# Heads in groups of four, bands of a sub-block in one operation, and softmax pieces between the blocks

## The chip, the cores and the metric

One core of a Trainium2 chip. The time is the device time of one execution in microseconds (us). Runs of the kernel before lie between 759.1 and 761.6 us. Engines are called as in the profile: PE is TensorE with PEld its weight loads, DVE is VectorE, ACT is ScalarE, POOL is GpSimd, SP is SyncE, which here only starts transfers.

## The reference

A causal convolution of seven taps whose weights are made per token and head by a softmax, then a feed-forward layer with a squared ReLU:

```python
# x (8, 4096, 192), weight_gen (8, 4096, 8 heads, 7 taps)
w = softmax(weight_gen, axis=-1)
out = np.einsum('bshk,bskhg->bshg', w, x_unf)      # x_unf: x at t-6 .. t, 24 channels a head
h = np.maximum(out.reshape(32768, 192) @ w_in, 0)  # w_in  (192, 2048)
return h * h @ w_out                               # w_out (2048, 192)
```

## The kernel before

The 32768 tokens are 64 sub-blocks of 512. From the second block on, a block is two sub-blocks. TensorE alternates between 16 units of the first product ("u"), the sums of the second product for the block before ("M") and one convolution ("C") for the block after:

```python
steady = "MuMuuu" * 3 + "MuuuMCu"
```

The convolution is done as a matrix product with banded matrices. DVE builds the bands of a sub-block from the softmax rows `wr` and a mask; they stand in `bd` by pairs of heads, so that the two heads of a pair alternate:

```python
def st_band(j, tiles):                       # tiles of 104 columns; called with (0,1), (2,3), (4,)
    shape = (P, HP * len(tiles), n // SL, 2 * SL)          # HP = H // 2
    nc.vector.tensor_tensor(out=bd_t[j][...], in0=wr_t[j][...].broadcast_to(shape),
                            in1=mask[...].broadcast_to(shape), op=AluOp.mult)

# st_conv: 120 matmuls a block, four side by side on different columns of the array
bd = bd_t[s][:, H * lo : H * hi].rearrange("p (g c e) -> p g e c", g=HP, e=2)
nc.tensor.matmul(out=yps[k // per][p0 : p0 + m, col + a : col + b],
                 lhsT=x_t[s][:, i, 32 * q : 32 * q + m],
                 rhs=bd[:, h // 2, h % 2, a - lo : b - lo],    # every second element: step two
                 start=True, stop=True, tile_position=(0, p0))
```

The softmax is made in pieces of eight rows (`exp` on ACT; `total`, `recip` and `scale` on DVE), placed at certain units of certain blocks. `exp` writes the heads of a group next to each other, `total` therefore reads the taps of one head at the step of the group, and `scale` needs one operation a group. The second product ends in `o_sum`, a copy on ACT and an add on DVE; there is one pair of PSUM buffers for it.

The softmax here doesn't subtract the row's maximum and nothing guards it: scores larger than these inputs give would overflow.

Of the kernel before, what the change touches and what calls it, by code (L numbers as in the profile page):

```python
# [9 lines left out]
def kernel(  # L10
# [25 lines left out]
    nc = tc.nc  # L36
# [5 lines left out]
    Dff = moe_w_in.shape[1]  # L42
    Dm = moe_w_out.shape[1]
    HK = H * KK
    HP = H // 2

    P = 128
    TB = 512
# [39 lines left out]
    NQ = Dff // WQ  # L88
    w_i = const.tile([P, WQ, 2, NQ + NQ // 2], f16, name="w_i")
    w_o = const.tile([P, NF, Dm], f16, name="w_o")  # L90
    mask = const.tile([P, P, 2], f16, name="mask")
    FIRST = 8
    PARTS = {0: (8, 8, 8, 8), 1: (8, 8, 16), 2: (16, 16)}
    v_big = const.tile([P, R + 2 * HALO, HP, SL, 2], f16, name="v_big")
    v_first = [
        const.tile([P, FIRST + 2 * HALO, HP, SL, 2], f16, name=f"v_first{i}") for i in (0, 1)
    ]

    def band_mask():

        nc.gpsimd.memset(mask, 1.0)
        for sign, base in ((1, 0), (-1, KK - 1)):
            nc.gpsimd.affine_select(
                out=mask, in_=mask, pattern=[[sign, P], [0, 2]], compare_op=AluOp.is_ge,
                fill=0.0, base=base, channel_multiplier=-sign,
            )

# [38 lines left out]
    class Softmax:  # L146
# [35 lines left out]
        def exp(self, lo, hi):  # L182

            if lo == 0:
                self.ex = self.tile(p_one, p_one, "ex", HK, "ex8").rearrange(
                    "p (r g k e) -> p r g k e", g=HP, k=KK, e=2
                )
                self.ssum, self.rcp = (
                    self.tile(p_sm, p_sm, n, H, n + "8").rearrange(
                        "p (r g e) -> p r g e", g=HP, e=2  # L190
                    )
                    for n in ("ssum", "rcp")
                )
            nc.scalar.activation(  # L194
                out=self.ex[:, lo:hi].rearrange("p r g k e -> p (r g) k e"),
                in_=self.wg[:, lo:hi].rearrange("p r (g e) k -> p (r g) k e", e=2),
                func=ActF.Exp,
            )

# [10 lines left out]
        def scale(self, lo, hi, eng):  # L210

            v = self.v
            while lo < hi:
                n = min(SL - lo % SL, hi - lo)
                for g in range(HP):
                    eng.tensor_tensor(  # L216
                        out=bass.AP(
                            tensor=v.tensor,
                            offset=v.offset + lo * H * SL + lo % SL * 2 + g * SL * 2,
                            ap=[list(v.ap[0]), [H * SL + 2, n], [H * SL, KK], [1, 2]],  # L220
                        ),
                        in0=self.ex[:, lo : lo + n, g],
                        in1=self.rcp[:, lo : lo + n, g].unsqueeze(2).broadcast_to((P, n, KK, 2)),
                        op=AluOp.mult,
                    )
                lo += n
# [64 lines left out]
        copy(out=x_t[j].rearrange("p t d -> p (t d)"), in_=x_st[j][:, 0 : NT * D])  # L291

    def wr_load(j):
        wr_t[j] = p_wr.tile([P, NT, HP, SL * 2], f16, name="wr")
        wr = wr_t[j].rearrange("p t g c -> p t (g c)")
        block_load(j, wr, vd_t[j // NBB], H * SL, nc.sync)

    def wr_load_sbuf(j, parts, order, engines):

        wr_t[j] = p_wr.tile([P, NT, HP, SL * 2], f16, name="wr")  # L300
        n = 0
        for i in order:
            t0 = max(j % NBB * TB + tile_start(j, i), 0)
            for s in parts:
                a, b = max(t0, s.t0), min(t0 + P, s.t0 + P * s.r)
                if a < b:
                    engines[n % len(engines)].dma_start(  # L307
                        out=wr_t[j][a - t0 : b - t0, i].rearrange("p g c -> p (g c)"),
                        in_=s.v[
                            (a - s.t0) // s.r : (b - s.t0) // s.r, HALO : HALO + s.r  # L310
                        ].rearrange("p r g c e -> p r (g c e)"),
                    )
                    n += 1

    def st_band(j, tiles):

        if j not in bd_t:
            bd_t[j] = p_bd.tile([P, H * TB], f16, name="bd")
        i = tiles[0]
        lo, hi, n = bounds[i], bounds[tiles[-1] + 1], bounds[i + 1] - bounds[i]  # L320
        shift = 0 if i == 0 and j % NBB == 0 else lo - tile_start(j, i)
        shape = (P, HP * len(tiles), n // SL, 2 * SL)
        nc.vector.tensor_tensor(  # L323
            out=bd_t[j][:, H * lo : H * hi].rearrange(
                "p (g m c) -> p g m c", g=shape[1], c=2 * SL
            ),
            in0=wr_t[j][:, i : tiles[-1] + 1]
            .rearrange("p t g c -> p (t g) c")
            .unsqueeze(2)
            .broadcast_to(shape),  # L330
            in1=mask[:, shift : shift + n]
            .rearrange("p (m c) e -> p m (c e)", c=SL)
            .unsqueeze(1)
            .broadcast_to(shape),
            op=AluOp.mult,
        )
# [35 lines left out]
    def st_conv(j):  # L372
# [7 lines left out]
            ps_h.tile([P, 2 * TB], f32, name="yp", tag="h") for _ in range(-(-NK // per))  # L380
        ]
        for later, s, i, q, half, a, b, base in conv_pieces(j):
            lo, hi = bounds[i], bounds[i + 1]
            _, ha, hb, pre = quads[q]
            m, h = (32, hb) if later else (pre, ha)
            bd = bd_t[s][:, H * lo : H * hi].rearrange("p (g c e) -> p g e c", g=HP, e=2)
            p0 = RT * half + 32 * (q % 2)
            k = q // 2
            col = th * (k % per) - base
            nc.tensor.matmul(  # L390
                out=yps[k // per][p0 : p0 + m, col + a : col + b],
                lhsT=x_t[s][:, i, 32 * q : 32 * q + m],
                rhs=bd[:, h // 2, h % 2, a - lo : b - lo],
                start=True,
                stop=True,
                skip_group_check=True,
                tile_position=(0, p0),
            )
# [72 lines left out]
            ],  # L471
        )

    def st_bands(j, part):

        groups = ((0,), (1,), (2, 3)) if j % NBB == 0 else ((0, 1), (2, 3))
        for tiles in (groups, ((NT - 1,),))[part]:
            st_band(j, tiles)

    with nc.allow_low_precision("fp16 matmul pipeline"), tc.manual_schedule():  # L480

# [54 lines left out]
        for i in (0, 2, 1, 3, 4):  # L536
            st_band(0, (i,))
        st_conv(0)
        s1.exp(0, s1.rh)
        st_bands(1, 0)  # L540
        st_bands(1, 1)
        x_cast(1, nc.vector.tensor_copy)
        s1.total(0, s1.rh)
        s1.recip(0, s1.rh)
        s1.scale(0, s1.rh, nc.vector)

        nc.gpsimd.memset(x_st[1][:, 0:1], 0.0)
        for q in range(4):
            load_w_out(q, 4)
        move_rows(s1)  # L550
        s2.load(nc.sync)
        nc.gpsimd.memset(v_big, 0.0)
        x_load(2)
        x_load(3)



# [7 lines left out]
        def at(j, u, kind, *args):  # L565
# [2 lines left out]
        PIECE = 8  # L568

        TIMES = {  # L570
            (0, 2): ((1, 7), (2, 1)),
            (0, 3): ((2, 15), (3, 1)),
            (1, 0): ((3, 15), (4, 1)),
            (1, 1): ((4, 15), (5, 1)),
            (1, 2): ((5, 9), (5, 15), (6, 1)),
            (2, 0): ((6, 15), (7, 1), (7, 9)),
            (2, 1): ((8, 1), (8, 15), (9, 1)),
            (3, 0): ((9, 9), (9, 15), (10, 9), (10, 15), (11, 1)),
        }

        EXP_AT = {1: 0, 7: 4, 9: 4, 15: 8}
        loads = {}
        for n, s in enumerate(parts[2:], 2):
            b, f = s.b, s.fb
            k = n - min(m for m, p in enumerate(parts) if p.b == b)
# [2 lines left out]
            )  # L588
            pieces = [(lo, min(lo + PIECE, s.rh)) for lo in range(0, s.rh, PIECE)]
            for (j, u), (lo, hi) in zip(times, pieces, strict=True):  # L590
                at(j, EXP_AT[u], "exp", s, lo, hi)
                at(j, u, "soft", s, lo, hi)
            if n > 2:
                loads.setdefault(times[0][0] - 1, []).append(s)
        for j in range(1, NBLK - 1):
            a = BLOCKS[j + 1][0]
            when = (1, 9, 5, 9)
            if j == 1:
                when = (1, 1, 3, 3)
            elif j == 2:  # L600
                when = (5, 6, 8, 9)
            elif j in (3, 4, 5):
                when = (5, 7, 9, 11)
            elif j == 6:
                when = (9, 9, 11, 11)
            for u, args in zip(when, ((a, 0), (a, 1), (a + 1, 0), (a + 1, 1))):
                at(j, u, "band", *args)

        stored, waiting = set(), []

# [11 lines left out]
        def run_fill(j, u):  # L622
            for kind, *args in fill.get((j, u), ()):
                if kind == "band":
                    st_bands(*args)
                    continue
                s, lo, hi = args
                if kind == "exp":
# [18 lines left out]

        FCS = (range(NF // 2), range(NF // 2, NF))
        for j, (sub, n) in enumerate(BLOCKS):
            for s in loads.get(j, ()):  # L650
                s.load(nc.sync)
            if j + 2 < NBLK:
                load_rows(j + 2)
            u = m = 0
            for step in orders.get(j, steady):
# [13 lines left out]
                    u += 1  # L669
                elif j + 1 < NBLK:  # L670
                    st_conv(j + 1)
            if 0 < j < NBLK - 2:
                for k in range(BLOCKS[j + 2][0], sum(BLOCKS[j + 2])):
                    x_load(k)

# [46 lines left out]
```

## Time and profile before

| | |
|---|---|
| time, median | 760.98 us |
| span of the profiled run | 759.8 us |
| packed block (convolution to convolution) | 22.55 us |
| convolution, 120 matmuls | 1.59 us |
| DVE busy | 631.2 us |

The instruction groups of the kernel before that the change touches (line, engine, operation, out<-in, shapes, count, then busy time and mean ns of one, then idle time before):

```profile
L323 DVE TENSOR_TENSOR bd<-wr,mask 128x1664 f16<-128x1664 f16 x119 | 116.5, 1018 | 2.2 <-DMA wr<-v_first 2.2
...
L390 PE MATMUL yp<-bd,xt 128*32 128x104 f16 x1524 | 36.2, 210 | 0.0
...
L216 DVE TENSOR_TENSOR v_big<-ex,rcp 128x112 f16<-128x112 f32 x104 | 21.7, 272 | 1.0
...
L194 ACT ACTIVATE ex<-wg 128x448 f32<-128x448 f32 x30 | 19.0, 633 | 0.0
...
L201 DVE TENSOR_REDUCE ssum<-ex 128x64 f32<-128x448 f32 x30 | 18.3, 610 | 0.0
```

The bands, the scale and the sum are on DVE (116.5, 21.7 and 18.3 us in these shapes, beside 337 us of squares), the exponential on ACT. The second line is on TensorE, which sets the time; its mean of 210 ns is one matmul from its start to its end, while the matmuls of a convolution follow each other every 11.6 ns, (1.59 - 0.21) us / 119. What a matmul costs is this distance to the next, which has to be read from the timeline: a row of n matmuls there contains n - 1 distances and one last matmul.

### The profile page before, as it was taken

The numbers are of one execution on the slowest core, as the hardware profiler recorded it, in microseconds if no ns is written. First come the engines' busy times: TensorE is split into PE (matmuls) and PEld (weight loads), VectorE is DVE, ScalarE is ACT, GpSimd is POOL, SyncE is SP. The second block draws the span as 40 slices with busy tenths as digits, with TensorE's granted clock in tenths as the row PEclk, the third lists the DMA queues.
The fourth block names the chain that finished last, engine by engine and source line by source line (L and its number), as shares of the span: only waits on it lengthen the run. The fifth ranks groups of instructions, "written<-read, shape, count | busy, mean of one in ns | idle before, by whom it ended". The sixth has DMA issues, their size and how long they took to land.

```text
span 759.8 us, 33723 instructions
## 1 busy us (share of the span) xinstructions
PE 741.8 (98%) x15266; PEld 561.0 (74%) x15266; DVE 631.2 (83%) x1119; ACT 623.8 (82%) x753; POOL 87.3 (11%) x126
## 2 busy tenths in 40 slices
PE   7899999999999999999999999999999999999998
PEld 3767777877877777777777777777777777777777
DVE  5888999898899988898888888888888887777853
ACT  3887888878888888888888888888888888888873
POOL 3522212011100110010100110001100011000000
PEclk9999999999999999999999999999999999999999
DMA  7844432546325544344445423454432454432311
GB/s 228 121 79 97 91 96 51 100 104 138 70 68 114 107 79 59 107 76 82 79 79 116 96 60 52 79 136 98 68 63 41 76 107 79 58 68 52 52 44 65
DMA packets 122395, 65.23 MB, mean 86 GB/s; under 512 B 83881, under 2 KB 118668, under 8 KB 121740
## 3 DMA queue, kind: packets, MB, share of 16 engines
q1 hardware_dynamic: 78012, 46.46, 21.4%
q0 software_dynamic: 44096, 16.53, 20.1%
q8 instruction: 119, 1.95, 1.1%
q14 instruction: 24, 0.20, 0.1%
q10 hardware_dynamic: 144, 0.10, 0.0%
HBM read 48.61 MB, written 28.70 MB: 102 GB/s over the span
## 4 chain that ended last, share of the span: by engine, by line
PE 87%; DVE 5%; issue 2%; DMA 1%; ACT 1%; POOL 0%; SPq 0%; POOLq 0%; DVEq 0%
PE o L447 42%; PE h L415 39%; PE yp L390 5%; DVE g L427 2%; DVE bd L323 1%; DMA xt<-in_x_dram 1%; DVE o_sb L462 1%; DMA wr<-v_first 0%; ACT o_sb L461 0%; ACT t L424 0%; DVE v_big L216 0%; DVE rcp L208 0%; DVE ssum L201 0%; POOL xt L277 0%; POOL xt L271 0%
## 5 line engine op out<-in xcount | busy, mean ns | idle before, releaser
L424 ACT ACTIVATE t<-h 128x1024 f16<-128x1024 f32 x512 | 497.1, 1026 | 72.7 <-PE h L415 71.0
L427 DVE TENSOR_TENSOR g<-t 128x1024 f16<-128x1024 f16 x512 | 336.7, 688 | 97.9 <-ACT t L424 96.0
L447 PEld LDWEIGHTS <-g 64*128 64x128 f16 x8192 | 351.5, 94 | 61.4 <-issue 9.7
L447 PE MATMUL o<-w_o,g 64*128 64x192 f16 x8192 | 384.9, 243 | 5.9 <-DVE o_sb L462 5.3
L415 PE MATMUL h<-y,w_i 64*128 64x512 f16 (+1 forms) x3168 | 378.8, 371 | 6.9 <-ACT t L424 5.1
L415 PEld LDWEIGHTS <-w_i 64*128 64x128 f16 x3168 | 164.5, 94 | 118.8 <-issue 9.4
L323 DVE TENSOR_TENSOR bd<-wr,mask 128x1664 f16<-128x1664 f16 (+2 forms) x201 | 158.2, 830 | 4.7 <-DMA wr<-v_first 4.7
L277 POOL DMA_DIRECT2D xt<-in_x_dram x62 | 51.3, 830 | 442.4 <-PE yp L390 419.5
L461 ACT COPY o_sb<-o 128x384 f32<-128x384 f32 x129 | 62.2, 482 | 33.0 <-PE o L447 33.0
L462 DVE TENSOR_TENSOR o_sb<-o,o_sb 128x384 f32<-128x384 f32 x129 | 71.3, 553 | 12.5 <-ACT o_sb L461 7.1
L401 ACT CAST y<-yp 128x1024 f16<-128x1024 f32 (+1 forms) x64 | 48.1, 802 | 15.3 <-PE yp L390 15.3
L390 PE MATMUL yp<-bd,xt 128*32 128x104 f16 (+8 forms) x3864 | 51.9, 208 | 0.2
L390 PEld LDWEIGHTS <-xt 128*32 128x32 f16 (+3 forms) x3864 | 46.1, 92 | 6.5 <-issue 5.4
L194 ACT ACTIVATE ex<-wg 128x448 f32<-128x448 f32 (+2 forms) x44 | 27.2, 618 | 6.6 <-DMA wg<-in_weight_gen_dram 6.6
L201 DVE TENSOR_REDUCE ssum<-ex 128x64 f32<-128x448 f32 (+2 forms) x44 | 26.2, 595 | 3.9 <-ACT ex L194 3.9
L216 DVE TENSOR_TENSOR v_big<-ex,rcp 128x112 f16<-128x112 f32 (+1 forms) x136 | 27.4, 265 | 1.2
L208 DVE RECIPROCAL rcp<-ssum 128x64 f32<-128x64 f32 (+2 forms) x44 | 23.7, 539 | 1.5
L307 POOL DMA_DIRECT2D wr<-v_first x31 | 16.9, 563 | 28.2 <-DVE v_first L216 28.2
L267 POOL DMA_DIRECT2D xt<-in_x_dram x7 | 3.8, 546 | 137.6 <-PE yp L390 137.6
L508 PE MATMUL wp<-warm 128*128 128x512 f16 x42 | 12.1, 459 | 1.3 <-DVE warm L500 1.3
L508 PEld LDWEIGHTS <-warm 128*128 128x128 f16 x42 | 4.7, 114 | 8.1 <-issue 3.8
L216 DVE TENSOR_TENSOR v_first<-ex,rcp 128x112 f16<-128x112 f32 (+1 forms) x48 | 9.1, 256 | 0.3
(17 smaller groups left out, 23.9 us busy)
## 6 DMA issues: line engine op xcount, KB each, us to landing
out_dram<-o_sb SPq DMA_DIRECT2D x63, 384.0 KB, 2.7
xt<-in_x_dram POOLq DMA_DIRECT2D x42, 240.0 KB, 6.0
wg<-in_weight_gen_dram SPq DMA_DIRECT2D x4, 1064.0 KB, 8.0
xt<-in_x_dram POOLq DMA_DIRECT2D x20, 192.0 KB, 6.4
wr<-vd SPq DMA_DIRECT2D x38, 80.0 KB, 5.3
vd<-v_big SPq DMA_DIRECT2D x5, 512.0 KB, 5.7
wg<-in_weight_gen_dram SPq DMA_DIRECT2D x6, 392.0 KB, 4.3
wg<-in_weight_gen_dram SPq DMA_DIRECT2D x3, 616.0 KB, 6.1
```

The lines of the kernel that those rows point to most:

```text
L194: nc.scalar.activation(out=self.ex[:, lo:hi].rearrange("p r g k e -> p (r g) k e"), in_=self.wg[:, lo:hi].rearrange("p r (g e) k -> p (r g ...
L216: eng.tensor_tensor(out=bass.AP(tensor=v.tensor, offset=v.offset + lo * H * SL + lo % SL * 2 + g * SL * 2, ap=[list(v.ap[0]), [H * SL + 2, ...
L277: eng.dma_start(out=dst[:, first:last], in_=ap)
L323: nc.vector.tensor_tensor(out=bd_t[j][:, H * lo : H * hi].rearrange("p (g m c) -> p g m c", g=shape[1], c=2 * SL), in0=wr_t[j][:, i : tile ...
L390: nc.tensor.matmul(out=yps[k // per][p0 : p0 + m, col + a : col + b], lhsT=x_t[s][:, i, 32 * q : 32 * q + m], rhs=bd[:, h // 2, h % 2, a - ...
L401: nc.scalar.copy(out=y[:, k0:k1, 0:th], in_=yp[:, 0 : (k1 - k0) * th].rearrange("p (k c) -> p k c", c=th),)
L415: nc.tensor.matmul(out=h[:, half, jj * th : (jj + 1) * th], lhsT=w_in_chunk(u * per + jj, slot, half), rhs=y_t[j][r0 : r0 + RT, k, 0:th], ...
L424: nc.scalar.activation(out=t1, in_=h, func=ActF.Relu)
L427: nc.vector.tensor_tensor(out=g, in0=t1, in1=t1, op=AluOp.mult)
L447: nc.tensor.matmul(out=oo[:, cc * Dm : (cc + 1) * Dm], lhsT=g[r0 : r0 + RT, cc * P : (cc + 1) * P], rhs=w_o[r0 : r0 + RT, fc, :], start=(f ...
L461: nc.scalar.copy(out=o_sb, in_=o[0][:, c])
L462: nc.vector.tensor_tensor(out=o_sb, in0=o[1][:, c], in1=o_sb, op=AluOp.add)
```

## The change

The intent: fewer and longer operations on DVE (one band operation for a sub-block instead of three, two scale operations a piece instead of four), softmax pieces away from the places where the add of the second product has to wait for them, and a start in which ACT is not held up by the second softmax part. The groups of four are what halves the number of scale operations. Cut to the core:

```diff
-    HP = H // 2
+    HE = 4
+    HG = H // HE
 ...                                    # 2 -> HE and HP -> HG in mask, v_big, wr, exp, total, scale
-            bd_t[j] = p_bd.tile([P, H * TB], f16, name="bd")
+            bd_t[j] = p_bd.tile([P, H * NT * STEP], f16, name="bd")
 ...
-            bd = bd_t[s][:, H * lo : H * hi].rearrange("p (g c e) -> p g e c", g=HP, e=2)
+            bd = bd_t[s][:, H * lo : H * hi].rearrange("p (g c e) -> p g e c", g=HG, e=HE)
-                rhs=bd[:, h // 2, h % 2, a - lo : b - lo],
+                rhs=bd[:, h // HE, h % HE, a - lo : b - lo],
 ...
-        groups = ((0,), (1,), (2, 3)) if j % NBB == 0 else ((0, 1), (2, 3))
-        for tiles in (groups, ((NT - 1,),))[part]:
-            st_band(j, tiles)
+        for tiles in (range(first), range(first, last), range(last, NT)):
+            if tiles:
+                st_band(j, tiles)
 ...                                    # the start
-        s1.exp(0, s1.rh)               # now before unit 4 of block 0
-        s1.total(0, s1.rh); s1.recip(0, s1.rh); s1.scale(0, s1.rh, nc.vector)   # now before unit 5
-        nc.gpsimd.memset(x_st[1][:, 0:1], 0.0)
         for q in range(4):
             load_w_out(q, 4)           # now earlier on its queue
-        move_rows(s1)
-        s2.load(nc.sync)               # now at unit 6 of block 0
-        x_load(2); x_load(3)           # now after block 0
 ...                                    # softmax pieces: unit 1 -> unit 0 in most places, others moved;
                                        # bands at units 1 and 5 (5 and 9 early on) instead of 1, 5, 9, 9
```

## The prediction

Numbers from the traces: 11.6 ns from matmul to matmul in the convolution; a clock of 0.83 in the window from 20 to 30 us, which holds the stop of 4.17 us, and 0.63 after the one of 1.48; and 0.52 ns for an element of the bands. The sum: 1 (start) + 1 (block 2 to 3) + 4 (blocks 5 to 10) = 6 us off 760.6, so 754.6, stated as 754, with the convolution at 0.

Three of its figures, with what the traces show beside them. The 42.7 ns of rival A are the 102.4 columns of a mean matmul: a matmul of 512 columns takes 377 ns and one of 192 columns 243, so (377 - 243)/320 = 0.42 ns a column and 42.9 ns. The 0.117 us under *Scale* are 112 elements: the operation takes 272 ns for 112 and, in the changed kernel, 388 for 224, so 0.116 us. The 1.7 us of lost clock are an estimate from the 0.63: after that stop 31 matmuls of the second product took 2.53 us and six of the first 1.58, elsewhere 1.48 (for 31 or 32) and 0.82.

> **What bounds the kernel now.** I read the page first, then the timeline of TensorE, then the waits and the timelines of VectorE (DVE) and ScalarE (ACT) where TensorE stood still, and last a table of windows for its clock. From the page:
>
> ```profile
> span 759.8 us, 33723 instructions
> PE 741.8 (98%) x15266; PEld 561.0 (74%) x15266; DVE 631.2 (83%) x1119; ACT 623.8 (82%) x753; POOL 87.3 (11%) x126
> ...
> PE 87%; DVE 5%; issue 2%; DMA 1%; ACT 1%; POOL 0%; SPq 0%; POOLq 0%; DVEq 0%
> ```
>
> TensorE is busy 98% of the span and carries 87% of the chain that ended last; DVE, which nearly all of the change is about, carries 5%. So a DVE instruction saved is worth only what TensorE waits for DVE. A busy PE need not be a dense one, so the timeline of TensorE decides (start, duration, engine, line, shape, count, idle before):
>
> ```profile
> 405.25 1.59 PE L390 MATMUL yp<-bd,xt 128*32 128x104 f16 x120
> 406.78 0.82 PE L415 MATMUL h<-y,w_i 64*128 64x512 f16 x6
> 407.43 1.48 PE L447 MATMUL o<-w_o,g 64*128 64x192 f16 x32
> ...
> 427.80 1.59 PE L390 MATMUL yp<-bd,xt 128*32 128x104 f16 x120
> ```
>
> From one convolution to the next is 22.55 us. A block holds 16 units of the first product at 0.647 us (1.94 us for three), 8 half sums of the second at 1.32 and one convolution of about 1.6: 10.35 + 10.56 + 1.6 = 22.5. An ordinary block is packed, and no saving on DVE can shorten it. What can be won is in blocks that take longer. I subtracted 22.55 from the distance between successive convolutions: the block from 56.98 us has 3.96 too much, those from 128.60, 152.13, 176.69, 200.18 and 245.78 have 0.98, 2.01, 0.94, 0.52 and 0.55 (5.0 together), the remaining ones 0.0 to 0.6. Most of the latter (2.0 us in all) show "issue" before a matmul and no other engine, about every 90 us, so I leave them as they are. The stops, with what ended them:
>
> ```profile
> 21.45 2.74 PE L415 MATMUL h<-y,w_i 64*128 64x256 f16 x24 [4.17 <-ACT t L424]
> ...
> 61.42 2.53 PE L447 MATMUL o<-w_o,g 64*128 64x192 f16 x31 [1.48 <-DVE o_sb L462]
> ...
> 131.77 1.48 PE L447 MATMUL o<-w_o,g 64*128 64x192 f16 x31 [0.65 <-DVE o_sb L462]
> ...
> 155.53 1.48 PE L447 MATMUL o<-w_o,g 64*128 64x192 f16 x31 [0.67 <-DVE o_sb L462]
> ```
>
> The first is ACT held up in its own order: the exponential of the second softmax part stands before the activations of the first units and waits 4.47 us for its weights, until 19.56 us. The others are the output sum: there is one pair of PSUM buffers for it, and the add that frees them stands on DVE behind bands, softmax pieces and a backlog of squares. A stop also costs afterwards (window, time, busy times of PE, PEld, DVE, ACT, POOL, clock, DMA share, GB/s):
>
> ```profile
> 61.40:66.00 4.60, 4.58 (x62) 4.10 (x63) 2.48 (x7) 1.46 (x3) 0.00 (x0) 0.63 1.18 183
> ...
> 128.60:152.10 23.50, 22.85 (x474) 19.35 (x472) 20.22 (x39) 19.52 (x25) 1.77 (x2) 1.00 0.43 82
> ```
>
> After the stop at 61.42 the clock is 0.63 for 4.6 us, a loss of 0.37 x 4.6 = 1.7 us on top of the 1.48. After the short ones it stays 1.00.
>
> [...] (1.59 - 0.21) us / 119 = 11.6 ns from matmul to matmul, four of which sit side by side, so 46.4 ns a group. No row before has step four on TensorE. [...] The trace shows 0.83 in the window with the 4.17 us stop, and 0.63 after 1.48 us of idleness with smaller gaps before it[...]. [...] (1018 - 584) ns / 832 elements = 0.52 ns. [...]
>
> **The change part by part.**
> *Bands.* Three operations of a plain sub-block (1664, 1664, 768 elements) become one of 4160. One operation has 1018 - 1664 x 0.52 = 150 ns of fixed time, but two in a row take 1.95 us, so the second adds 0.94, and the fixed cost that counts is 0.94 - 0.87 = 0.07 us. Removed: 2 x 0.07; added: 64 elements x 0.52 = 0.03. Saved 0.11 us a sub-block, some 7 us over 64. One operation then blocks DVE for about 2.3 us in one go, at units 1 and 5 instead of 1.95 at 1 and 5 and 1.02 at 9.
> *Scale.* Four operations of 112 elements take 0.83 us in a row; the fixed part is about 0.19 - 0.117 = 0.07 each, so two of 224 elements save 0.15 us a piece, 46 pieces, 7 us.
> DVE falls from 631 to about 617 us. In packed blocks this is idle time gained and nothing else.
> *Start.* The exponential of the second part moves behind four activations, its sums behind unit 4's square, and the second-product weights are loaded some 7 us earlier. The 4.17 us stop should go: I work out the second convolution at 19.3 to 20.6 instead of 24.12. But little of it stays. The cast of x still stands before the squares and waits for its load (18.57 us), and the weight load, now among x and softmax loads with DMA busy 82% there, may delay both. The softmax work (about 2.7 us of DVE) now lies in front of the last squares of block 0, and bands of the third and fourth sub-block still need the moved rows. By working DVE forward I get those rows 1 us later to 2 us later than before, and the third convolution at 36.1 to 37.8, where it was 36.90. Block 2 is then bound by ACT and DVE anyway: 16 activations at 0.93, casts 1.4, copies and exponentials 2 give 18.3 of its 20.1 us. I give the start 1 us (-1.5 to 2.5).
> *Block 2 to 3.* The second piece of the third part comes one unit earlier and the bands are shorter, so the add that ended at 61.36 should end at about 59 to 60. The stop shrinks from 1.48 to at most 1 and may keep its clock: 1 us more (0 to 3).
> *Blocks 5 to 10.* In block 5 DVE has 16 squares (9.6), 4 adds (1.9), three softmax pieces (5.8) and bands of two sub-blocks (5.3): 22.6 in 22.55. After it, 9.6 + 1.9 + 5.3 + 5.0 = 21.8. Pieces move from unit 1 to 0 and away from 9, so piece and band no longer stand together in front of an add. I expect 4 of the 5.0 us back (2.5 to 5).
> *Convolution.* Same matmuls and the same columns: 0 if step four streams.
> Sum: 1 + 1 + 4 = 6 us, so 760.6 - 6 = 754.6; I state 754.
>
> **The rivals.** A: step four halves the stream. Each convolution then takes 30 x 42.7 ns = 1.28 us more, 31 of them 40 us: about 795 us, 4% slower. A partial loss of 10% is only 4 us and would eat most of the gain. For: [...] four matmuls read at once. Against: [...] ACT's exponential reads its input at a step of 28 bytes already and still costs only (633 - 527)/112 = 0.95 ns an element, and nobody would regroup the heads to lose 4%. One in ten. B: the change does nothing, because DVE is not on the path: 759 to 762. For: 83% busy and a packed steady block; the start gives its gain back. Against: the named stops on the DVE add. One in five. C: the 2.3 us bands make new stops. In the window of 5.23 us between two adds DVE would have 2.3 + 4 x 0.6 + 0.5 = 5.2 us of work. But the add stands ahead of the band and the next half sum comes three units later, so there is 1.9 us of slack, which I think is enough; if not, some 0.3 us a block, 5 to 9 us, and no gain. D: all goes well: no stop after 60 us and none of the lost clock: 2.5 + 3 + 5 = 10.5, so 750; with all of the start kept as well perhaps 747.
> The sum of the DVE fp32 reads at step four (16 bytes[...]) might double the 0.46 us of a reduction's elements; 44 of them make at most 20 us of DVE, which would bring C nearer.
>
> **Range and chances.** The centre is 754; D bounds it below at 748, and B with a small loss in the convolution above at 762. Faster by over 2% means under 745.4, beyond all the stops that I count: 0.04. Slower by over 2% needs rival A nearly in full: 0.08. Within 2%: 0.88.
>
> **What would show it.** Right: a convolution of 120 still at 1.59 us on TensorE's timeline; packed blocks still 22.55 us apart; bands of 4160 elements near 2.3 us; no stop of 4.17 at 21 us; the wait for the output add falling from 5.3 us to 1 or less; DVE near 617 us. Wrong: convolutions of 1.7 us or more (A); new waits for the add at every block (C); the reduction of 448 elements above 0.61 us; the block from 57 us still near 26 us (no gain before 83 us).

## The result, and the profile after

The changed kernel takes 802.48 us (801.62 to 804.66), the kernel before 760.98 in the same rounds: ratio 1.0554, interval 1.0526 to 1.0583. Ratios here are the mean time of one kernel's fast runs over the mean of the other's fast runs of the same rounds, so they are not quite the ratio of the medians. The result is correct. The prediction, 754 with a range of 748 to 762, was wrong. From the page of the changed kernel:

```profile
span 802.9 us, 33518 instructions
...
PE 783.8 (98%) x15266; PEld 586.6 (73%) x15266; DVE 632.7 (79%) x915; ACT 640.9 (80%) x753; POOL 88.1 (11%) x125
...
PE o L451 41%; PE h L419 39%; PE yp L394 11%; DMA wg<-in_weight_gen_dram 2%; ACT t L428 1%; DMA w_st<-in_moe_w_in_dram 1%; DVE g L431 1%; SPq L308 0%; DVE bd L326 0%; SPq L119 0%; DVE ssum L202 0%; ACT w_i L533 0%; SPq L278 0%; ACT ex L195 0%; DVE v_first L217 0%
```

The number of TensorE instructions is the same (15266), but its busy time has grown by 42 us, and in the chain that ended last the convolution (yp) has gone from 5% to 11%. DVE has 204 instructions fewer and is still busy for 632.7 us, 1.5 more than before. The timeline of TensorE in the changed kernel shows the size (start, duration, engine, line, shapes, count):

```profile
428.42 3.01 PE L394 MATMUL yp<-bd,xt 128*32 128x104 f16 x120
431.36 0.82 PE L419 MATMUL h<-y,w_i 64*128 64x512 f16 x6
432.02 1.48 PE L451 MATMUL o<-w_o,g 64*128 64x192 f16 x32
...
452.38 3.00 PE L394 MATMUL yp<-bd,xt 128*32 128x104 f16 x120
```

The other matmuls take what they took. The convolution takes 3.01 us instead of 1.59, and a packed block 23.96 instead of 22.55: 31 x 1.41 = 43.7 us. From matmul to matmul it is (3.01 - 0.27) us / 119 = 23.0 ns, before 11.6. The groups of the changed kernel that answer to those above:

```profile
L326 DVE TENSOR_TENSOR bd<-wr,mask 128x4160 f16<-128x4160 f16 x42 | 97.3, 2316 | 1.7 <-DMA wr<-v_first 1.7
...
L394 PE MATMUL yp<-bd,xt 128*32 128x104 f16 x1524 | 55.6, 274 | 6.3 <-DVE xt L292 4.9 <-ACT xt L292 1.4
...
L195 ACT ACTIVATE ex<-wg 128x448 f32<-128x448 f32 x30 | 30.4, 1013 | 4.9 <-DMA wg<-in_weight_gen_dram 4.9
L202 DVE TENSOR_REDUCE ssum<-ex 128x64 f32<-128x448 f32 x30 | 28.6, 954 | 0.0
...
L217 DVE TENSOR_TENSOR v_big<-ex,rcp 128x224 f16<-128x224 f32 x52 | 18.0, 388 | 1.0
```

The bands are as expected (2316 ns). But the sums (on DVE) and the exponentials (on ACT) over a group of four take 1.6 times as long as over pairs. All sums together take 40.8 us instead of 26.2, which is why DVE has won nothing.

The start has become worse too. TensorE's stops in the changed kernel, in the brackets:

```profile
24.88 1.61 PE L394 MATMUL yp<-bd,xt 128*32 128x104 f16 x72 [4.92 <-DVE xt L292]
...
44.31 1.46 PE L419 MATMUL h<-y,w_i 64*128 64x256 f16 x12 [4.88 <-ACT t L428]
...
48.27 3.02 PE L394 MATMUL yp<-bd,xt 128*32 128x104 f16 x120
```

The stop of 4.17 us is gone, and there are two of nearly 5 in its place, so that the third convolution starts at 48.27 us, 11.4 later than before (in the profiled run, the slowest of the four). After 65 us TensorE has no stop of 0.2 us or more: the stops at the add of the second product, which the change was after, are away. One could think from this that the new schedule failed and the convolution only suffers beside the long band operations. That is the rival in the first runs.

### The profile page after: what moved, and what is told of

Read it like the earlier page. It is cut to its first block, busy times and chain, and to the rows that moved or that the text cites. A ratio compares the mean times of both kernels' runs of the same rounds, so it can differ in the third digit from the quotient of the medians.

```text
span 802.9 us, 33518 instructions
## 1 busy us (share of the span) xinstructions
PE 783.8 (98%) x15266; PEld 586.6 (73%) x15266; DVE 632.7 (79%) x915; ACT 640.9 (80%) x753; POOL 88.1 (11%) x125
## 4 chain that ended last, share of the span: by engine, by line
PE 92%; DMA 3%; ACT 2%; DVE 1%; SPq 1%; issue 1%; ACTq 0%
PE o L451 41%; PE h L419 39%; PE yp L394 11%; DMA wg<-in_weight_gen_dram 2%; ACT t L428 1%; DMA w_st<-in_moe_w_in_dram 1%; DVE g L431 1%; SPq L308 0%; DVE bd L326 0%; SPq L119 0%; DVE ssum L202 0%; ACT w_i L533 0%; SPq L278 0%; ACT ex L195 0%; DVE v_first L217 0%
## 5 line engine op out<-in xcount | busy, mean ns | idle before, releaser
L451 PEld LDWEIGHTS <-g 64*128 64x128 f16 x8192 | 346.6, 94 | 59.7 <-DVE g L431 1.6
L451 PE MATMUL o<-w_o,g 64*128 64x192 f16 x8192 | 380.8, 243 | 1.0 <-DVE g L431 0.7
L419 PEld LDWEIGHTS <-w_i 64*128 64x128 f16 x3168 | 150.3, 94 | 133.2 <-issue 14.7
L326 DVE TENSOR_TENSOR bd<-wr,mask 128x4160 f16<-128x4160 f16 (+3 forms) x89 | 149.5, 1703 | 5.3 <-DMA wr<-v_first 5.3
L394 PE MATMUL yp<-bd,xt 128*32 128x104 f16 (+8 forms) x3864 | 96.7, 272 | 6.3 <-DVE xt L292 4.9
L394 PEld LDWEIGHTS <-xt 128*32 128x32 f16 (+3 forms) x3864 | 88.5, 110 | 12.1 <-DVE xt L292 5.2
L195 ACT ACTIVATE ex<-wg 128x448 f32<-128x448 f32 (+2 forms) x44 | 43.5, 989 | 11.3 <-DMA wg<-in_weight_gen_dram 11.3
L202 DVE TENSOR_REDUCE ssum<-ex 128x64 f32<-128x448 f32 (+2 forms) x44 | 40.8, 927 | 3.0 <-ACT ex L195 3.0
L217 DVE TENSOR_TENSOR v_big<-ex,rcp 128x224 f16<-128x224 f32 (+1 forms) x68 | 22.7, 374 | 1.2
L217 DVE TENSOR_TENSOR v_first<-ex,rcp 128x224 f16<-128x224 f32 (+1 forms) x24 | 7.4, 359 | 0.3
```

What stands on the lines that cost most here:

```text
L195: nc.scalar.activation(out=self.ex[:, lo:hi].rearrange("p r g k e -> p (r g) k e"), in_=self.wg[:, lo:hi].rearrange("p r (g e) k -> p (r g ...
L202: nc.vector.tensor_reduce(out=self.ssum[:, lo:hi].rearrange("p r g e -> p (r g) e"), in_=self.ex[:, lo:hi].rearrange("p r g k e -> p (r g) ...
L326: nc.vector.tensor_tensor(out=bd_t[j][:, H * lo : H * (lo + len(tiles) * n)].rearrange("p (g m c) -> p g m c", g=shape[1], c=HE * SL), in0 ...
L419: nc.tensor.matmul(out=h[:, half, jj * th : (jj + 1) * th], lhsT=w_in_chunk(u * per + jj, slot, half), rhs=y_t[j][r0 : r0 + RT, k, 0:th], ...
L451: nc.tensor.matmul(out=oo[:, cc * Dm : (cc + 1) * Dm], lhsT=g[r0 : r0 + RT, cc * P : (cc + 1) * P], rhs=w_o[r0 : r0 + RT, fc, :], start=(f ...
```

## The experiments

Theory R: the loss is the read at step four by the convolution's matmuls. Rival S: it is the new schedule, with its start, or the long band operations beside the matmuls.

**Pairs.** The changed kernel with one number set back:

```diff
-    HE = 4
+    HE = 2
```

> The changed kernel with the heads in pairs again; bands in one operation, the new schedule and the new start stay. Theory R (the read at step four): a convolution of 120 matmuls is back at 1.59 us, packed blocks at 22.55 us; 31 x 1.41 us come off 802.5, so 757 to 761 us, and the loss at the start stays. Rival S (the new schedule, with its start, or the long band operation beside the matmuls): convolution stays near 3.0 us or the time near 800.

Measured: 757.38 us (756.02 to 759.55), ratio to before 0.9966 (0.9946 to 0.9987). The convolution takes 1.59 us again and packed blocks 22.55. With pairs, all the rest of the change gains a little.

**Four.** The kernel before with groups of four and nothing else (HP becomes H // 4, and 2 becomes 4, at all places of the layout).

> The kernel before with nothing but the heads in groups of four; bands, schedule and start as before. Theory R: convolution 3.0 us, packed blocks 23.97, about 761 + 43 = 800 to 806 us. Rival S: 759 to 763 us. The exponential of 448 elements should go from 633 to about 1013 ns and the sum from 610 to about 954 if the grouping alone does it.

Measured: 801.19 us (800.74 to 801.67), ratio 1.0541 (1.0524 to 1.0559). The convolution takes 3.00 us, the exponential of 448 elements 1014 ns and the sum 959. So the grouping alone loses 41 us, with the old schedule, the old start and short bands; S falls.

**Step two.** The grouping changes more than the read. Here the groups of four stay, and only the matmuls' view of the band tile is another (a wrong result):

```diff
-            bd = bd_t[s][:, H * lo : H * hi].rearrange("p (g c e) -> p g e c", g=HG, e=HE)
+            bd = bd_t[s][:, H * lo : H * lo + 2 * (hi - lo)].rearrange("p (c e) -> p e c", e=2)
-                rhs=bd[:, h // HE, h % HE, a - lo : b - lo],
+                rhs=bd[:, h % 2, a - lo : b - lo],
```

> The changed kernel as it is, with groups of four, but the convolution's matmuls read the band tile at step two (the result is wrong on purpose; same number of columns, same instructions). Theory R: 1.59 us a convolution, 758 to 763 us, with the exponential and the sum still slow (1013 and 954 ns). Rival: the grouping costs by other means (slow exponentials and sums, long bands): 3.0 us a convolution or still over 790 us.

Measured: 760.24 us (758.31 to 760.53), ratio 0.9996 (0.9980 to 1.0012); exponential 1018 ns, sum 956. The convolution on TensorE's timeline:

```profile
402.97 1.59 PE L394 MATMUL yp<-bd,xt 128*32 128x104 f16 x120
```

So the read step of 3864 matmuls makes 802.48 - 760.24 = 42.2 us, and the slow exponentials and sums make no more than the 2.9 us to the run with pairs.

**What is paid: in proportion, or beyond a threshold?** If the time of a read is in proportion to the elements that it passes over, steps three and eight follow from the 23.0 ns of step four: three quarters of it, 17.3, and twice, 46. These are the same edit with 3 and 8 in the place of 2, also wrong on purpose, one look each (state unknown, clock 0.993 and 0.998).

> The changed kernel, the convolution reading its bands at step three, 6 bytes (wrong result on purpose). [...] 69 ns, 17.3 ns a matmul, 2.3 us a convolution. If there is a threshold (free up to some step, half rate beyond): 11.6 or 23 ns, 1.6 or 3.0 us.

> The same at step eight, 16 bytes[...] (wrong result on purpose). [...] 184 ns a group, 46 ns a matmul, 5.7 us a convolution, some 885 us in all. Threshold at half rate: 3.0 us and 802 us.

Measured: 779.5 and 883.39 us. The convolution on TensorE's timeline, at step three:

```profile
413.21 2.32 PE L394 MATMUL yp<-bd,xt 128*32 128x104 f16 x120
```

and at step eight:

```profile
413.31 5.77 PE L394 MATMUL yp<-bd,xt 128*32 128x104 f16 x120
```

With one matmul's own length taken off (238 and 364 ns), that is (2.32 - 0.24)/119 = 17.5 ns and (5.77 - 0.36)/119 = 45.5 ns from matmul to matmul, where the proportion predicted 17.3 and 46. There is no jump to half rate: from step three to eight the time grows as the elements that a read passes over. In each of the four matmuls side by side, with 102.4 columns in the mean, it is 4 x 17.5/(3 x 102.4) = 0.23 ns for each element passed over at step three, 0.22 at step four and 0.22 at step eight. No run has a longer step, and none shows by what means the read is slower.

**Whose limit?** In the convolution four matmuls read from the same partitions at once: 4 x 11.6 = 46.4 ns for four of 102.4 columns in the mean, against 42.9 for one alone at 0.42 ns a column. In the second product two run side by side, on different halves of the partitions: 1.32 us / 16 = 82.5 ns for two of 192 columns, against 80.4 for one alone. I made that one read its weights (here they are the moving operand, `rhs`) at steps four, eight and two, in the kernel before (wrong):

```diff
-                        rhs=w_o[r0 : r0 + RT, fc, :],
+                        rhs=w_o_at(r0, fc),      # 192 columns at step 4, 8 or 2, from fc or the last that fits
```

> The kernel before, the second product reading its weights at step four (wrong result on purpose). Here two matmuls run side by side on different halves of the partitions[...]. If the limit is one that the four streams of a partition share[...]: 43 ns, below the 80 ns of streaming, so 1.32 us for 32 matmuls as before and 760 us. If each stream has its own limit[...]: 173 ns a pair, 2.8 us for 32, about 760 + 4096 x 0.09 = 1130 us.

> The same with the second product's weights at step eight (wrong result on purpose)[...]. Shared limit: 86 ns a pair instead of 82.5, 1.38 us for 32 matmuls, 760 to 780 us. Limit of each stream: 345 ns a pair, 5.5 us for 32, about 1840 us.

Its figures are in proportion, too: 173 ns is the 4 x 23.0 = 92 ns of a matmul at step four, times 192/102.4 columns; 43 is a quarter of that, if four streams share one limit.

Measured: 1113.86 and 2088.9 us, one run each. TensorE's timeline at step four:

```profile
513.94 2.91 PE L452 MATMUL o<-w_o,g 64*128 64x192 f16 x32
516.67 2.12 PE L415 MATMUL h<-y,w_i 64*128 64x512 f16 x18
```

From start to start 32 matmuls take 2.73 us, 171 ns a pair and 171/(4 x 192) = 0.22 ns for each element passed over. Each stream is limited by itself: a single one in a partition took the same 0.22 ns as each of the four. At step eight:

```profile
502.10 5.62 PE L452 MATMUL o<-w_o,g 64*128 64x192 f16 x32
507.54 1.46 PE L415 MATMUL h<-y,w_i 64*128 64x512 f16 x6
```

and a window of the same run (window, time, busy times of PE, PEld, DVE, ACT, POOL, clock, DMA share, GB/s):

```profile
300.00:400.00 100.00, 100.00 (x674) 37.18 (x672) 33.37 (x59) 29.99 (x35) 2.16 (x3) 0.64 0.13 30
```

5.44 us for 32, 340 ns a pair, again 0.22 ns an element passed over. In this run the clock was granted at 0.64 in that window, 0.666 in the mean. The first product slowed as well (1.46 us for six matmuls instead of 0.82), and the total went past the 1840 that I expected. The time of an element passed over was the same 0.22 ns in this run, with its mean clock of 0.666, and at step four, where the clock was 0.998 in the mean.

> The kernel before, the second product reading its weights at step two (wrong result on purpose). [...] 85.4 ns a pair, just above the 82.5 of streaming, so 1.37 us for 32 and 760 + 4096 x 0.003 = 772 us. [...]

Measured: 769.11 us (767.74 to 771.31), ratio 1.0120 (1.0100 to 1.0141). TensorE's timeline:

```profile
503.04 1.54 PE L452 MATMUL o<-w_o,g 64*128 64x192 f16 x32
504.40 2.12 PE L415 MATMUL h<-y,w_i 64*128 64x512 f16 x18
```

1.36 us from start to start instead of 1.32: 85.0 ns a pair, where half of the 171 of step four is 85.4 (2 x 192 x 0.222). So step two is already a hair above the 82.5 of step one.

> The changed kernel, the convolution reading its bands one after the other (wrong result on purpose). [...] 758 to 761 us as at step two (760.2). If step two still paid something, some 0.1 to 0.2 us a convolution less: 754 to 757.

Measured, again in the changed kernel and wrong: 759.99 us (759.63 to 761.75), ratio 1.0002 (0.9987 to 1.0018). The convolution is 1.54 us instead of 1.59, the packed block 22.50 instead of 22.55. As expected, there is next to nothing below step two; the time doesn't tell it from step two.

**What the rest of the change is worth.** With pairs, the start of before put back (second softmax part, weight load and first x loads where they stood):

> As the run with pairs, and also the start of before (second part's softmax, weight load of the second product and first x loads where they were). If the new start costs what the trace of the changed kernel shows at the third convolution (48.27 against 36.90 us, a part of it from slower exponentials and convolutions), 6 to 9 us less than the pairs alone: 749 to 753. If the start is given back later anyway: within 2 us of the pairs alone.

Measured: 754.02 us (753.84 to 754.53), ratio 0.9920 (0.9905 to 0.9935). The new start costs 3.4 us, less than I expected; two of TensorE's stops in this kernel answer to the waits for the add:

```profile
41.40 1.48 PE L451 MATMUL o<-w_o,g 64*128 64x192 f16 x31 [0.61 <-DVE o_sb L466]
...
60.72 1.48 PE L451 MATMUL o<-w_o,g 64*128 64x192 f16 x31 [0.62 <-DVE o_sb L466]
```

There were eight before (5.3 us), and now these two (1.2). The later one was 1.48 us long before, and the clock fell after it (0.63); here the clock is 1.00 from 61 to 66 us.

Then the one line that held the weight load, put back into the run with pairs and its new start:

```diff
         x_cast(1, nc.vector.tensor_copy)
+        nc.gpsimd.memset(x_st[1][:, 0:1], 0.0)
         for q in range(4):
             load_w_out(q, 4)
```

> The run with pairs (757.4 us), with the one line of before put back that holds the second product's weight load until the x of the second sub-block is cast. If that load, among the x and softmax loads, is what delayed the new start (x of the second sub-block cast at 23.75 us instead of 18.57), the cast comes at about 19.5 us, the second convolution near 20, and the time is 749 to 754 us, at or below the run with the old start (754.0). If it is something else in the new start: 756 to 758.

Measured: 753.52 us (752.30 to 756.46), ratio 0.9910 (0.9895 to 0.9924). DVE's cast of x, the run with pairs first:

```profile
23.75 0.66 DVE L292 CAST xt<-x_st 128x960 f16<-128x960 f32 x1 [6.87 <-DMA x_st<-in_x_dram]
```

and with the hold:

```profile
18.86 0.66 DVE L292 CAST xt<-x_st 128x960 f16<-128x960 f32 x1 [2.01 <-DMA x_st<-in_x_dram]
```

The weight load had indeed delayed the x load by 4.9 us, and the second convolution moves from 24.47 to 19.58. The median falls by 3.9 us. The two profiled runs don't show this gain: they span 754.1 and 754.3 us (the one with the hold is the slowest of its five, that of pairs the fastest of its four), and the third convolution starts at 41.80 instead of 42.38, because another stop comes later in the same start. TensorE with the hold:

```profile
38.38 1.47 PE L419 MATMUL h<-y,w_i 64*128 64x256 f16 x12 [4.93 <-ACT t L428]
```

There ACT waits for the inputs of the third softmax part, 5.3 us. The change has put this exponential one unit earlier, but that alone is not the cause: the run with the old start has it at the same unit, and there it runs at 34.19 without a wait. In both the load is issued at about the same time (28.74 with the old start, 29.12 here). Why ACT waits for it in one and not in the other was not tested, and I didn't mend it; 753.5 and 754.0 are the fastest versions here, and are not told apart.

**Bands alone.** The kernel before, with the bands of a sub-block in one operation at the unit of the first:

> The kernel before with one part of the change alone: the bands of a sub-block in one operation, at the units where the first of them stood; pairs, schedule and start as before. If the bands themselves earned what pairs with the old start gained (6.2 us): 753 to 756. If the new places of the softmax pieces and bands earned it: 758 to 761. If long bands alone make new stops: above 761.

Measured: 761.20 us (761.00 to 762.58), ratio 1.0013 (0.9996 to 1.0030): no gain. TensorE waits for the add eight times (6.3 us) as before (5.3). So it is not the shorter band work, but the new places of pieces and bands, perhaps only together with it, that take the stops away.

## Why the prediction was wrong

*What bounds the kernel, packed blocks, DVE off the path*: right. TensorE is busy throughout the packed blocks in all runs, and the bands alone took DVE from 631.2 to 624.8 us busy and moved nothing.

*The convolution, "0 if step four streams"*: this is the step that failed, and it alone takes the time out of the range (760.24 us with nothing but the read put back to step two). Step four doesn't stream. Rival A had half the stream (23.0 ns instead of 11.6) and nearly the size: 1.28 us a convolution, 40 us; measured 1.42 and 42 to 44. I gave it one in ten. Two arguments misled me. One took step four as free from a rule that no trace shows. In the runs a matmul's stream takes about 0.22 ns for each fp16 element that it passes over, and a column is due every 0.42 ns ((377 - 243)/320, from the 512 and 192 columns of the two products before), so 1.9 elements in the time of a column. So step two is at the edge, and at step four a matmul took 23.0 ns instead of 11.6. The other was ACT's exponential, which reads at a step of 28 bytes for 0.95 ns an element. But it alternates between two heads and goes on by 4 bytes in each, and an engine with 0.95 ns for an element says nothing about one with 0.42. The trace before already had a warning: 46.4 ns a group where 102.4 columns at 0.42 ns are due in 42.9. I drew no chance from it. That nobody would regroup the heads to lose 4% is no argument about hardware, and it was false.

*Scale, "7 us"*: the operations were halved as worked out, but the sums took it back. I had named it as a risk (at most 20 us): the sum's elements now cost (954 - 753)/112 = 1.79 ns instead of (610 - 495)/112 = 1.03, with 753 and 495 the means of the operation of 336 elements. Sums are 40.8 us in place of 26.2, and DVE ended at 632.7, not 617.

*Start, "1 us (-1.5 to 2.5)"*: wrong in sign. I had named the cause, the weight load among the x and softmax loads, and taken it as up to 2 us; it delayed the cast of x by 4.9. The wait of ACT for the third part's inputs (4.89 us in the changed kernel) was in no term of mine. With pairs the new start costs 3.4 us against the old. What the grouping adds is not shown: in the profiled runs with groups of four and the new start the third convolution starts at 43.2 to 48.3 us, and not by how long a convolution takes (48.15 at step one with 1.54 us, 43.21 at step two with 1.59).

*Block 2 to 3, 1 us (0 to 3), and blocks 5 to 10, 4 us (2.5 to 5)*: mechanism right, sizes too small. In the run with pairs and the old start, the stretch from the third to the fifth convolution is 43.00 us (38.16 to 81.16) instead of 46.59, so 3.6 us; from the fifth to the last it is 632.90 instead of 638.39, so 5.5 us; before the third, 1.3 us are lost (38.16 instead of 36.90; the runs with the old start lie between 36.9 and 39.4). The profiled runs differ by 8.2 us in their spans, the medians by 6.2, and the median of 754.0 is what I had predicted for the whole change. That is luck: nothing came from the start there, and the two other parts were larger. In the changed kernel itself the stops are away as well, but its longer convolutions cost far more than they gave.

*Rival C, new stops by bands of 2.3 us*: no such stop after 65 us, neither in the changed kernel nor in the run with pairs, whose blocks are as short as before. *Rival B*: close to what the long bands do alone.

## What to carry to other kernels

A layout that saves operations on a spare engine can cost the bound engine more: look first at who reads the tile, and set the elements that its read passes over per column, at 0.22 ns each for a matmul in fp16 here, against the 0.42 ns of a column. A matmul's moving operand in fp16 is nearly free here at step two (85.0 ns a pair instead of 82.5) and pays in proportion from three to eight (17.5, 23.0 and 45.5 ns a matmul at three, four and eight, instead of 11.6); longer steps were not run. And that a read at a step is free has to be shown at the rate of the engine in question, best with a run that alters the read step alone and lets the result be wrong.

## What stays open

- The sum on DVE took 1.79 ns an element at a step of 16 bytes in fp32, and 1.03 at 8 bytes. No run separates the cause.
- The exponential on ACT: reading two heads alternately it took 0.95 ns an element, reading four in turn (1013 - 822)/112 = 1.71, with the same 28 bytes between heads.
- The run whose second product read at step eight was granted a clock of 0.666 though TensorE was shown busy all the time (100%), the run at step four 0.998. One run each.
